# A retention layer followed by a bilinear feed-forward: how the first unit, w_out and the later loads are brought in

## The chip, the cores and the metric

The kernel runs on one core of a Trainium2 chip. The metric is the device time of one execution in microseconds (us); the median of 4 runs of the kernel before is 337.08 us (336.23 to 338.5). A core has five engines that run their own instruction lists and wait for each other by semaphores: PE (matrix products; its weight loads are shown as PEld), DVE and ACT (elementwise work), POOL (elementwise work, and here the issuer of nearly all loads) and SP (here the issuer of the stores and of transposes by DMA). PE's results stand in PSUM, which the program divides into eight banks, and other engines copy them out.

## The reference

For every batch b and head h, with q, k, v of 576 rows of 64 numbers (8 batches, 8 heads):

```python
scores = scale * np.matmul(q, k.transpose(0, 1, 3, 2))
Dmat = np.where(rel >= 0, gamma[:, None, None] ** rel[None, :, :], 0.0)
ret = scores * Dmat[None, :, :, :]
attn_out = np.matmul(ret, v)
x = attn_out.transpose(0, 2, 1, 3).reshape(4608, 512)
out = ((x @ w_a) * (x @ w_b)) @ w_out       # w_a, w_b: 512 x 1536, w_out: 1536 x 512
```

`rel` is the row minus the column, and gamma is 1 - 2^(-5-h). So each head is causal linear attention whose weight decays with distance, and its result goes through a feed-forward layer in which two products are multiplied with each other. Everything is float32 outside; the kernel computes in bfloat16 with float32 sums.

## The kernel before

The decay gamma^(row-column) is split into a factor for the row, put on q's side, and one for the column, put on v. A step of 64 rows then needs three things: its own masked scores times v, the state (the sum of k^T v over all earlier steps of the batch) times q, and the update of the state. Tokens are handled in chunks of 128 rows, in units of two chunks, and the feed-forward in blocks of 512 tokens: `ffn_ab` makes hT = (w_a x)(w_b x) by 12 slices F of d_ff (lines 414 and 422 are its products, 419 ACT's copy of the first, 427 DVE's multiplication), `ffn_out` multiplies hT with w_out (line 453) and stores the result.

The first 512 tokens, the "fresh" units 0 and 1 of 256 tokens each, have code of their own, for PE can do nothing before they are in. `load_fresh_qk` and `load_fresh_v` bring them in so that a partition holds two neighbouring tokens, called even and odd (`e`). For each unit PE transposes q and k (line 492), ACT and DVE copy them out of PSUM (614, 617, 618, 626, 630), PE makes the scores (549), DVE masks them with `keep2` (561), v is scaled with `vs_all` (`fresh_vscale`, line 479: for unit 0 on DVE in two halves of heads, for unit 1 on POOL), PE adds k^T v into `kv_sum` (`fresh_kv`, line 514), ACT copies that state (521), PE multiplies state with q (`fresh_from_state`, 527) and masked scores with v (`fresh_stage2`, 572), and xT is copied out (583, 586, 588). q's factor of unit 0 is `qs0`, four exponentials on ACT (206), multiplied in by DVE at line 614. `idle_products` are products of a tile of zeros that give PE something to do while it waits for loads, and `settled` is one such product that waits for a state.

The order on every engine is the order in which the program is written: nothing reorders it. POOL's list decides when loads start. It issues q, k and half of v of unit 0 (the other half is SP's), unit 1, w_a and w_b in slices of d_ff (`load_w`, 118), the whole of w_out (`load_wo`, 124) and then chunks 4 to 9 (`load_v` 110, `load_qk` 102). Loads to bfloat16 are converted on the way. A DMA issued by POOL waits for the landing of the eighth DMA that POOL issued before it.

Later units are woven into the feed-forward by a list `todo` of (cost, function, arguments). `run` adds up the cost of the feed-forward products (1.0 for a product 512 wide), and at each edge between groups calls what is due. `first` computes state times q and scores of a unit (`stage1`), `second` the rest (`stage2`), `kv` the state update (294), `transposes` the transposed q and k, on PE for chunks 4 to 7 (275, into a bank of the pool `ps_ffn`, which has 4 banks), by DMA from SP for the others. `ps_x` and `ps_o` have 2 banks each. `later` holds small steps that `pop` hands out one at a time.

## Time and profile before

| | |
|---|---|
| median of 4 runs | 337.08 us (336.23 to 338.5) |
| the profiled execution's own time | 335.46 us |
| its span, first to last instruction | 333.7 us |
| PE busy | 322.5 us, 97% of the span, 3746 products |
| DVE, POOL, ACT busy | 165.5, 143.6, 112.6 us |
| mean granted clock of PE | 0.993 |
| moved by DMA | 40.94 MB, mean 123 GB/s |
| product of 512 columns, start to start | 0.86 us for four |

The page of a profile cuts the span in 40 slices of 8.3 us and gives the busy share of each engine in tenths, and the clock that PE was granted. Its chain of waits is followed back from the last instruction. A line of the timeline is: start, duration of the merged run of instructions, engine, line of the kernel, operation, tile written and tiles read, shape, count, and in brackets how long the engine had been idle and what released it. A line of the waits is: who waited for whom, microseconds in total, times, and the longest.

### The profile page before, as it was taken

How to read it: one execution, taken by the hardware profiler on the slowest of the kernel's cores; microseconds unless marked ns; L12 is line 12 of the kernel's file. 1: busy time of each engine (PE TensorE's matmuls, PEld its weight loads, DVE VectorE, ACT ScalarE, POOL GpSimd, SP SyncE). 2: the span in 40 equal slices, each digit the busy share in tenths (PEclk: the TensorE clock that was granted, in tenths of full speed). 3: DMA queues.
4: the chain of work that ended last, by engine and by line, in shares of the span. 5: the costliest groups of instructions: out<-in, count | busy, mean ns of one | idle time of the engine just before them, and what ended most of it. 6: DMA issues, size and time to landing. Idle time of an engine off the chain costs nothing.

```text
span 333.7 us, 8838 instructions
## 1 busy us (share of the span) xinstructions
PE 322.5 (97%) x3746; PEld 166.9 (50%) x3746; DVE 165.5 (50%) x324; ACT 112.6 (34%) x233; POOL 143.6 (43%) x176
## 2 busy tenths in 40 slices
PE   6989989989999999999999999999999999999995
PEld 2664346877544454444444444454445444444443
DVE  6754345757643555446435644464455534444321
ACT  4737523545143214332333223322323133213321
POOL 8786298797666895308350855072000000000000
PEclk9799999999999999999999999999999999999999
DMA  9999999999999999907999599339801600020002
GB/s 140 206 154 194 217 190 242 175 127 173 187 230 165 125 133 214 173 5 101 109 200 102 87 148 251 24 65 137 181 0 33 128 34 1 17 81 31 2 31 94
DMA packets 116151, 40.94 MB, mean 123 GB/s; under 512 B 102992, under 2 KB 109392, under 8 KB 116112
## 3 DMA queue, kind: packets, MB, share of 16 engines
q0 software_dynamic: 80688, 23.34, 67.7%
q1 hardware_dynamic: 35280, 16.95, 26.6%
q8 instruction: 29, 0.48, 0.6%
q10 hardware_dynamic: 144, 0.10, 0.1%
q14 instruction: 10, 0.08, 0.1%
HBM read 37.75 MB, written 9.44 MB: 141 GB/s over the span
## 4 chain that ended last, share of the span: by engine, by line
PE 84%; DMA 10%; POOL 3%; issue 1%; DVE 0%; ACT 0%; POOLq 0%; ACTq 0%
PE po L453 26%; PE pa L414 25%; PE pb L422 25%; DMA wo_sb<-in_moe_w_out_dram 4%; DMA vf<-in_v_dram 2%; DMA wa_sb<-in_moe_w_a_dram 2%; PE o L339 2%; PE o L381 2%; PE kv L294 2%; DMA qk<-in_k_dram 1%; PE sc L359 1%; POOL fqk L141 1%; PE po L442 1%; POOL fvb L479 1%; POOL wb_sb L118 1%
## 5 line engine op out<-in xcount | busy, mean ns | idle before, releaser
L427 DVE TENSOR_TENSOR hT<-ha,pb 128x512 bf16<-128x512 bf16 (+1 forms) x123 | 76.5, 622 | 99.8 <-PE pb L422 84.6
L414 PE MATMUL pa<-xT,wa_sb 128*128 128x512 bf16 (+1 forms) x492 | 113.8, 353 | 1.6 <-issue 1.2
L422 PE MATMUL pb<-xT,wb_sb 128*128 128x512 bf16 (+1 forms) x492 | 113.5, 353 | 0.0
L419 ACT CAST ha<-pa 128x512 bf16<-128x512 f32 (+1 forms) x123 | 65.6, 533 | 123.9 <-PE pa L414 122.8
L453 PE MATMUL po<-wo_sb,hT 128*128 128x512 bf16 x420 | 95.5, 380 | 0.6 <-DMA wo_sb<-in_moe_w_out_dram 0.6
L422 PEld LDWEIGHTS <-wb_sb 128*128 128x128 bf16 x492 | 48.1, 98 | 45.3 <-issue 0.3
L414 PEld LDWEIGHTS <-wa_sb 128*128 128x128 bf16 x492 | 46.9, 98 | 46.1 <-issue 2.1
L256 POOL TENSOR_TENSOR vb<-vf,vs_all 128x512 bf16<-128x512 f32 x30 | 31.5, 1060 | 77.4 <-PE o L339 44.5
L453 PEld LDWEIGHTS <-hT 128*128 128x128 bf16 x420 | 39.1, 98 | 45.3 <-DMA wo_sb<-in_moe_w_out_dram 1.1
L462 ACT COPY osb<-po 128x512 f32<-128x512 f32 x18 | 10.5, 585 | 74.8 <-PE po L453 74.8
L102 POOL DMA_DIRECT2D qk<-in_q_dram x36 | 31.1, 868 | 6.7 <-DMA wo_sb<-in_moe_w_out_dram 6.2
L110 POOL DMA_DIRECT2D vf<-in_v_dram x36 | 31.9, 888 | 1.2 <-DMA wb_sb<-in_moe_w_b_dram 1.2
L102 POOL DMA_DIRECT2D qk<-in_k_dram x36 | 31.2, 874 | 0.6 <-DMA wa_sb<-in_moe_w_a_dram 0.4
L367 DVE TENSOR_TENSOR sT<-sc,keep 128x512 bf16<-128x512 f32 x32 | 20.6, 685 | 12.1 <-PE sc L359 12.1
L398 DVE TENSOR_TENSOR xT<-o,qs 128x512 bf16<-128x512 f32 x32 | 20.6, 685 | 11.9 <-PE o L339 11.8
L307 DVE TENSOR_TENSOR s<-kv,s 128x256 f32<-128x256 f32 x49 | 20.6, 420 | 5.9 <-ACT sbf L317 4.6
L317 ACT CAST sbf<-s 128x256 bf16<-128x256 f32 x56 | 21.1, 406 | 3.1 <-DVE s L305 2.7
L464 DVE COPY osb<-po 128x512 f32<-128x512 f32 x17 | 11.7, 687 | 19.3 <-PE po L453 19.3
L339 PE MATMUL o<-qkT,sbf 64*64 64x64 bf16 x456 | 12.1, 195 | 0.1
L339 PEld LDWEIGHTS <-sbf 64*64 64x64 bf16 x456 | 8.2, 107 | 5.7 <-issue 5.5
L381 PEld LDWEIGHTS <-vb 64*64 64x64 bf16 x512 | 6.4, 108 | 6.6 <-issue 6.6
L381 PE MATMUL o<-sT,vb 64*64 64x64 bf16 x512 | 8.2, 195 | 0.0
(75 smaller groups left out, 128.3 us busy)
## 6 DMA issues: line engine op xcount, KB each, us to landing
out_dram<-osb SPq DMA_DIRECT2D x35, 256.0 KB, 4.9
vf<-in_v_dram POOLq DMA_DIRECT2D x29, 256.0 KB, 6.2
qk<-in_q_dram POOLq DMA_DIRECT2D x28, 128.0 KB, 6.6
qk<-in_k_dram POOLq DMA_DIRECT2D x28, 128.0 KB, 6.9
wo_sb<-in_moe_w_out_dram POOLq DMA_DIRECT2D x1, 1536.0 KB, 14.3
wa_sb<-in_moe_w_a_dram POOLq DMA_DIRECT2D x6, 192.0 KB, 6.5
wb_sb<-in_moe_w_b_dram POOLq DMA_DIRECT2D x6, 192.0 KB, 7.3
vf<-in_v_dram POOLq DMA_DIRECT2D x8, 128.0 KB, 7.6
```

The costliest lines, as they stand in the source:

```text
L102: nc.gpsimd.dma_start(t[r0:r0 + n, w, :].rearrange("p (h d) -> p h d", h=H), src[b, :, s0:s0 + n, :].rearrange("h s d -> s h d"))
L110: nc.gpsimd.dma_start(t[r0:r0 + n, :].rearrange("p (h d) -> p h d", h=H), v[b, :, s0:s0 + n, :].rearrange("h s d -> s h d"))
L256: eng.tensor_tensor(vb.rearrange("p (h d) -> p h d", h=H), vf.rearrange("p (h d) -> p h d", h=H), vs[:, i % PER, :].unsqueeze(2).to_broadc ...
L307: nc.vector.tensor_tensor(new, ps[s][:, ci], last_sum[0], op=ALU.add)
L317: nc.scalar.copy(sb, new)
L339: nc.tensor.matmul(o[s][half(c), ci, j, :], st[half(r), p, :], qkt_of[i][half(r), 0, p, half(s)], start=start, stop=True, skip_group_check ...
L381: nc.tensor.matmul(o[s][half(c), ci, j, :], vb[half(s), 64 * h:64 * h + 64], sT[half(s), h % 2, ci, h // 2, :], start=False, stop=True, sk ...
L414: nc.tensor.matmul(pa[:, 0:n], wa_sb[:, c, fs], xT[:, c, tok0:tok0 + n], start=(c == 0), stop=(c == NC - 1))
L419: nc.scalar.copy(ha[:, 0:n], pa[:, 0:n])
L422: nc.tensor.matmul(pb[:, 0:n], wb_sb[:, c, fs], xT[:, c, tok0:tok0 + n], start=(c == 0), stop=(c == NC - 1))
L427: nc.vector.tensor_tensor(hT[:, F, off:off + n], ha[:, 0:n], pb[:, 0:n], op=ALU.mult)
L453: nc.tensor.matmul(po, hT[:, F, u * 128:(u + 1) * 128], wo_sb[:, F, :], start=(F == 0), stop=(F == NF - 1))
```

## The change

- q of unit 0 is loaded by SP as float32 into `fq32` and scaled to bfloat16 by DVE in two halves of heads, with row factors `qv` (16 numbers a partition, one exponential) in place of `qs0`. Its transposes are copied out in halves by ACT and DVE, without a factor.
- POOL's first DMA is k of unit 0, the second is all of v of unit 0. v's even part is scaled by POOL, its odd part by ACT in eight operations of one head each. For unit 1 the even part is DVE's and the odd part ACT's. On POOL's list the scaling stands between w_a and w_b of the first slice.
- `idle` is float32: 9 products of 512 columns become 2 of 512 and 1 of 128, and the later 1 and 2 become 1 of 128 and 1 of 256. `idle_beside` is new: two such products of 256 columns ahead of `fresh_kv(1, 0)`. Products with the zero state of unit 0 are left away.
- k of unit 1 is transposed after `fresh_kv(0, 1)` and copied in halves by ACT and DVE. The mask's row numbers come from POOL.
- w_out is loaded in three parts, with chunk 4 and chunk 5 between them; `ffn_out_parts` does block 0 in the same three parts and holds four banks of `ps_ffn`. Transposes of chunks 4 and 5 go to `ps_x`.
- The costs in `todo` change: chunk 4 is transposed earlier, `kv` of the third and fourth unit and the loads of chunks 10 to 13 come later.

```diff
+    fq32 = const.tile([128, 2 * DM], FP32)
...
+    def load_fresh_qk(u, w):
+        t = nat.tile([128, 2, DM], BF16, tag="qk", name="fqk")
+        flat = t.rearrange("p a b -> p (a b)")
+        if u == 0 and w == 0:
+            nc.sync.dma_start(fq32.rearrange("p (h x) -> p h x", h=H),
+                              fresh_src(w, u))
+        else:
+            nc.gpsimd.dma_start(flat.rearrange("p (h x) -> p h x", h=H),
+                                fresh_src(w, u))
+        fresh[u, w] = flat.rearrange("p (h e d) -> p h e d", h=H, e=2)
+        return flat
...
-    load_fresh_v(0, 0, 4, nc.sync)
-    load_fresh_qk(0)
+    load_fresh_qk(0, 0)
+    load_fresh_qk(0, 1)
     ramp(idx[:, 0:512], [[1, 512]], 0, 0)
     ramp(posf[:, 0:4], [[1, 2], [256, 2]], 0, 2)
     ramp(posf[:, 4:4 + MID + 1], [[128, MID + 1]], 0, 1)
-    load_fresh_v(0, 4, 8, nc.gpsimd)
+    for c in (0, 1):
+        ramp(rowf[64 * c:64 * c + 64, 0:2], [[1, 2]], 0, 2)
+    load_fresh_v(0, 0, 8, nc.gpsimd)
+    load_fresh_qk(1, 0)
     ramp(posf[:, 4 + MID + 1:NPOS], [[128, PER - MID - 1]], 64, 1)
-    load_fresh_qk(1)
+    load_fresh_qk(1, 1)
     load_fresh_v(1, 0, 8, nc.gpsimd)
-    load_w(0, 128)
-    load_w(128, 384)
-
-    idle = const.tile([128, 512], BF16)
+    load_w(0, 128, (0,))
+
+    idle = const.tile([128, 512], FP32)
...
-    qs0 = const.tile([128, HP, 256], FP32)
-    for p in range(HP):
-        nc.scalar.activation(qs0[:, p], idx[:, 0:256], AF.Exp,
-                             bias=biasq[:, 0:1], scale=lgq[:, p:p + 1])
+    qv = const.tile([128, 2, H], FP32)
+    nc.vector.tensor_tensor(
+        qv, posf[:, 0:4:2].unsqueeze(2).to_broadcast([128, 2, H]),
+        lgv.unsqueeze(1).to_broadcast([128, 2, H]), op=ALU.mult)
+    nc.scalar.activation(qv, qv, AF.Exp, bias=biasq[:, 0:1], scale=-1.0)
...
-    def transposes(i, by_dma):
+    def transposes(i, by_dma, place=ps_ffn, tag="ab"):
...
+    def ffn_out_parts(blk, parts):
+        hT = hT_of.pop(blk)
+        po = [ps_ffn.tile([128, 512], FP32, tag="ab", name="po")
+              for _ in range(4)]
+        for f0, f1 in parts:
+            for u in range(4):
+                for F in range(f0, f1):
+                    nc.tensor.matmul(po[u], hT[:, F, u * 128:(u + 1) * 128],
+                                     wo_sb[:, F, :],
+                                     start=(F == 0), stop=(F == NF - 1))
+                    if F < f1 - 1:
+                        yield 1.0, False
+                if f1 == NF:
+                    store(512 * blk + 128 * u, po[u], u)
+                pop()
+                yield 1.0, True
...
-        for e in (0, 1):
+        for e in es:
+            if eng is nc.scalar:
+                for h in range(h0, h1):
+                    nc.scalar.activation(
+                        fv[u][e][:, 64 * h:64 * h + 64],
+                        vf2[:, u, 128 * h + 64 * e:128 * h + 64 * e + 64],
+                        AF.Copy, bias=0.0,
+                        scale=vs_all[:, 2 * e + u, h:h + 1])
+                continue
...
-                fresh_from_state(u, h, s, j == 0)
+                if u or s:
+                    fresh_from_state(u, h, s, j == 0)
...
+    def idle_beside(n):
+        for _ in range(n):
+            nc.tensor.matmul(kv_sum[:, 256:512], idle[:, 0:128],
+                             idle[:, 0:256], start=False, stop=True,
+                             skip_group_check=True)
...
-    idle_products(9)
-    fresh_vscale(0, 0, 4, nc.vector)
+    idle_products(2)
+    idle_products(1, 128)
+    make_qs(256, 512)
+    make_keep2()
+    for h0 in (0, 4):
+        nc.vector.tensor_tensor(
+            fresh[0, 0][:, h0:h0 + 4],
+            fq32.rearrange("p (h e d) -> p h e d", h=H, e=2)[:, h0:h0 + 4],
+            qv.rearrange("p e h -> p h e")[:, h0:h0 + 4].unsqueeze(3)
+            .to_broadcast([128, 4, 2, D]), op=ALU.mult)
     q_out, k_out = fresh_tiles(0)
-    tq = fresh_transposed(0, 0, 0, HP, AB)
-    idle_products(1)
+    tq = [fresh_transposed(0, 0, 0, 2, AB), fresh_transposed(0, 0, 2, 4, X)]
+    idle_products(1, 128)
+    nc.scalar.copy(q_out[:, 0:2], tq[0].rearrange("p c e t -> p c t e"))
+    nc.vector.tensor_copy(q_out[:, 2:4], tq[1].rearrange("p c e t -> p c t e"))
     tk = [fresh_transposed(0, 1, 0, 2, AB), fresh_transposed(0, 1, 2, 4, X)]
-    make_keep2()
-    nc.vector.tensor_tensor(q_out, tq.rearrange("p c e t -> p c t e"),
-                            qs0.rearrange("p c (t e) -> p c t e", e=2),
-                            op=ALU.mult)
     nc.scalar.copy(k_out[:, 0:2], tk[0])
     nc.vector.tensor_copy(k_out[:, 2:4], tk[1])
-    make_qs(256, 512)
-    idle_products(2)
-    fresh_vscale(0, 4, 8, nc.vector)
+    fresh_vscale(0, 0, 8, nc.gpsimd, (0,))
+    fresh_vscale(0, 0, 8, nc.scalar, (1,))
+    load_w(0, 128, (1,))
+    load_w(128, 384)
+    idle_products(1, 256)
     fresh_scores(0, (X, AB))
     fresh_kv(0, 0)
     q_out, k_out = fresh_tiles(1)
     tq = fresh_transposed(1, 0, 0, HP, AB)
     nc.scalar.copy(q_out, tq.rearrange("p c e t -> p c t e"))
-    tk = fresh_transposed(1, 1, 0, HP, AB)
     fresh_state1(0)
     fresh_kv(0, 1)
-    nc.scalar.copy(k_out, tk)
-    fresh_vscale(1, 0, 8, nc.gpsimd)
+    tk = [fresh_transposed(1, 1, 0, 2, AB), fresh_transposed(1, 1, 2, 4, X)]
+    nc.scalar.copy(k_out[:, 0:2], tk[0])
+    nc.vector.tensor_copy(k_out[:, 2:4], tk[1])
...
     fresh_stage2(0)
+    fresh_vscale(1, 0, 8, nc.vector, (0,))
+    fresh_vscale(1, 0, 8, nc.scalar, (1,))
     fresh_scores(1, (X, O))
     run_all(ffn_ab(0, 0, 256, 0, 1))
+    idle_beside(2)
     fresh_kv(1, 0)
...
-    load_wo(0, NF)
...
-    load(*range(4, 10))
-    todo = [(110, vscale, (4, nc.vector)), (110, vscale, (5, nc.vector)),
-            (110, transposes, (4, False)), (112, transposes, (5, False)),
+    PARTS = ((0, 4), (4, 8), (8, NF))
+    load_wo(*PARTS[0])
+    load(4)
+    load_wo(*PARTS[1])
+    load(5)
+    load_wo(*PARTS[2])
+    load(*range(6, 10))
+    todo = [(90, vscale, (4, nc.vector)),
+            (90, transposes, (4, False, ps_x, "x")),
+            (108, vscale, (5, nc.vector)),
+            (112, transposes, (5, False, ps_x, "x")),
             (116, kv, (units[0], nc.scalar)),
             (128, first, (0,)), (136, second, (0,)),
-            (136, vscale, (6, nc.gpsimd)), (136, vscale, (7, nc.gpsimd)),
-            (142, transposes, (6, False)), (148, transposes, (7, False)),
-            (152, kv, (units[1], nc.scalar)),
+            (136, vscale, (6, nc.gpsimd)), (142, vscale, (7, nc.gpsimd)),
+            (144, transposes, (6, False)), (150, transposes, (7, False)),
+            (154, kv, (units[1], nc.scalar)),
             (174, first, (1,)), (184, second, (1,)),
-            (150, transposed, (2,)), (151, scale_v, (2,)),
-            (152, load, (10, 11)),
-            (184, kv, (units[2], nc.scalar)),
-            (191, transposed, (3,)), (192, scale_v, (3,)),
-            (193, load, (12, 13)),
-            (207, kv, (units[3], nc.scalar)),
-            (232, first, (2,)), (244, second, (2,))]
+            (146, transposed, (2,)), (165, scale_v, (2,)),
+            (178, load, (10, 11)),
+            (194, kv, (units[2], nc.scalar)),
+            (206, transposed, (3,)), (214, scale_v, (3,)),
+            (216, load, (12, 13)),
+            (218, kv, (units[3], nc.scalar)),
+            (236, first, (2,)), (246, second, (2,))]
...
-    run(ffn_out(0))
+    run(ffn_out_parts(0, PARTS))
```

## The prediction

> **What bounds the kernel now.** First the page, for where PE is not busy. PE is at nine tenths or more from the fifth slice of 8.3 us on, bar two; the chain that ended last is PE for 84%, DMA for 10%. So the time is PE's work plus PE's waits, and only two stretches have waits: the first 24 us, and 38 to 68 us.
>
> ```profile
> PE   6989989989999999999999999999999999999995
> PEclk9799999999999999999999999999999999999999
> ...
> PE 84%; DMA 10%; POOL 3%; issue 1%; DVE 0%; ACT 0%; POOLq 0%; ACTq 0%
> ```
>
> Second PE's waits, then PE's timeline around the three that stand after 24 us.
>
> ```profile
> PE pa L414 <- issue: 1.2, 1, 1.2
> ...
> PE tp L275 <- DMA qk<-in_k_dram: 1.1, 1, 1.1
> PE po L453 <- DMA wo_sb<-in_moe_w_out_dram: 0.6, 1, 0.6
> ...
> 38.36 1.03 PE L422 MATMUL pb<-xT,wb_sb 128*128 128x512 bf16 x4
> 40.03 3.63 PE L453 MATMUL po<-wo_sb,hT 128*128 128x512 bf16 x16 [0.65 <-DMA wo_sb<-in_moe_w_out_dram]
> 43.49 1.12 PE L275 MATMUL tp<-identity,qk 128*128 128x128 bf16 x12
> 45.70 0.40 PE L275 MATMUL tp<-identity,qk 128*128 128x128 bf16 x4 [1.09 <-DMA qk<-in_k_dram]
> ...
> 66.46 0.50 PE L414 MATMUL pa<-xT,wa_sb 128*128 128x256 bf16 x3
> 68.18 0.28 PE L414 MATMUL pa<-xT,wa_sb 128*128 128x256 bf16 x1 [1.21 <-issue]
> ```
>
> Idle time is counted from a modelled end; the loss is read from start to start. Four 512-wide matmuls start every 0.86 us, so the first po was due at 39.22 and came at 40.03: 0.8 lost. Four transposes take 0.22, so the last four were due at about 44.4 and came at 45.70: 1.3. At 66.46 three of four matmuls run and the fourth, due at 66.8, comes at 68.18: 1.4, with no releaser. Sum 3.5 us.
>
> Why were the loads late? POOL's timeline: the q load of chunk 5 is issued only when w_out, one DMA of 1536 KB, has landed. The queue holds eight DMAs, and the whole of w_out sat in one place.
>
> ```profile
> 33.22 0.91 POOL L110 DMA_DIRECT2D vf<-in_v_dram  x1 [1.02 <-DMA wb_sb<-in_moe_w_b_dram]
> 40.28 0.88 POOL L102 DMA_DIRECT2D qk<-in_q_dram  x1 [6.16 <-DMA wo_sb<-in_moe_w_out_dram]
> ```
>
> The 1.4 us: the page lists 29 packets, 0.48 MB, on queue q8 "instruction", 16 KB each, against 7,492 rows of PE and PEld: one packet for some 258 rows. In the packet list one starts at 65.6 and takes 1.25, just ahead of the hole. PE had gone through the 256 rows before it in 3.3 us (a state product and two groups of 64x64 products stand close together there), the shortest such stretch of the trace.
>
> Last the prologue, by windows of the clock's own steps (columns: stretch, length, busy us of PE, PEld, DVE, ACT and POOL, granted clock, DMA share, GB/s).
>
> ```profile
> 5.00:8.42 3.42, 1.58 (x34) 1.02 (x33) 2.83 (x8) 1.44 (x3) 3.42 (x5) 1.00 1.63 216
> 8.42:11.83 3.41, 3.41 (x74) 2.36 (x70) 2.68 (x6) 2.93 (x6) 2.90 (x6) 0.50 1.55 247
> 11.83:15.24 3.41, 2.69 (x113) 2.11 (x112) 1.76 (x4) 2.81 (x4) 1.98 (x3) 1.00 1.53 188
> ```
>
> A stretch with PE 46% busy is followed by one at half clock. The profiled execution took 335.46 us: span 333.7 and 1.8 around it. The median of the runs is 337.08, 1.6 more; I carry differences over to the median unchanged.
>
> **The change part by part.** All times are us from the span's start.
>
> *q, and scores of unit 0.* Before, SP's 256 KB of v landed 2.9 after an issue at 0.74; its packets ran 1.3 of that. Twice the bytes: 4.9, and 0.3 for sharing with k from 3.5 on: 5.2. DVE then scales q in two operations of 0.69 (row L256, same shape): halves at 5.9 and 6.5. k, now POOL's first DMA (row L141: 5.1 from an issue at 1.26, so 6.4), pays 0.5 for q's share: 6.9. Transposes of k 0.70, a copy 0.59: scores at about 8.4 instead of 9.57. This gain of 1.2 is worth nothing by itself: v is late next. Gone from ACT's way are four qs0 exponentials (0.49 each) and from DVE's the 1.23 of L614; they hid behind DMAs.
>
> *v of unit 0.* It is second on POOL. Its 512 KB follow k by 1.3 (twice the 0.6 by which 256 KB of v trailed k, 8.0 to 8.6) to 2.0 (unit 1: k 11.5, v 13.5): 8.2 to 8.9; I take 8.6. Even parts go to POOL: one L479 operation, 1.05, begun 0.3 after landing (L118 at 13.81 after 13.53): done at 9.95. Behind this wait on POOL's queue stand the issues of wb(0:128), wa and wb(128:384), and all weights after them; they have cover, since POOL's two operations on unit 1's v (14.44 to 16.49) go, and the load of wa(384:768) starts near 14.5, not 16.43. Odd parts go to ACT: eight activations 128x64. Nearest row: L235 128x64, two in 0.77, start to start 0.34, with two pointer operands; L200 128x32 with none takes 0.23 against 0.43. The new ones have one, so halfway, 0.26 each, 2.1 in all (bounds 0.16 and 0.34: 1.3 and 2.8): done at 10.75. The last product of kv(0,0) ends at 10.85, before it was 11.05: **-0.2**. From there to the first pa the steps keep their rows; eight zero-state products of 0.02 go.
>
> *v of unit 1.* pa and pb of F=0 end 5.3 after kv(0,0) (16.37-11.05), at 16.15. Before, kv(1,0) began at 16.45. Now DVE scales the even part (0.69, hidden), ACT the odd part in 2.1 after its copy of xT (14.93 before, 14.7 now): 16.8. PE itself first runs two idle_beside products. No fp32 product is in the trace: from one bf16 product of that width (0.11) to, by the column counts that the diff trades (512 bf16 columns for 128 fp32), four (0.43). I take four, the dearer end for this sum: 0.86, PE there at 17.0. **+0.5** for kv(1,0) and all behind it. Prologue's bounds: -0.15 (v at 8.2, activations at 0.16) to +1.65 (v at 8.9, activations at 0.34 in both units).
>
> *The other idle products.* 9x512 become 2x512 and 128 in fp32, and the later 1x512 and 2x512 become 128 and 256: at four each the same fill. They end near 5.3, before q's first half: 0. If dearer, 0.6 is covered.
>
> *w_out in thirds, chunks 4 and 5 between.* Weights end near 30.2 (32.2 before, minus 2.0). A third is 2.5 (512 KB at the 207 GB/s of 34 to 38 us), a chunk's loads 2.7 (39.98 to 42.73). So third 1 lands at 32.7, chunk 4 at 35.4, third 2 at 37.9, chunk 5 at 40.6, third 3 at 43.1. PE asks at about 39.7 for the first two, 43.7 for chunk 5, 44.3 for third 2, 48.4 for third 3: 2.8 or more to spare. **-0.8 and -1.3.** The three extra issues are 1.0 each of POOL, hidden under DMA time. The four po banks are held until the last third; their copies (0.59, 0.69) end 0.9 after it, and the fourth bank is needed 1.3 after.
>
> *Transposes of 4 and 5 in ps_x.* kv of unit 4,5 now needs that bank. In before the copies ended 1.47 after the transposes began (45.70 to 47.17); kv comes 1.3 after: **+0.3** (0 to 0.6).
>
> *Rows of PE.* kv of units[2] goes from 184 to 194, out of second(1)'s edge, and some 35 rows fewer precede it. The 256 rows at the old hole then take about 5.6 by the rows' durations, the shortest elsewhere 4.3: **-1.4** (0 if the hole only moves).
>
> *Loads held back.* POOL's order of instructions there is unchanged, so 0 (plus or minus 0.3).
>
> Sum: -0.2-0.8-1.3+0.3-1.4 with the +0.5 in place of the -0.2: 0.5-0.8-1.3+0.3-1.4 = **-2.7**; 335.46 becomes 332.8, the median 337.08 becomes **334.4**.
>
> **Two rules weighed.** The Trainium skill, "TensorE: Matmul & The Clock Gate", Part 1, has the clock fall after one idle window of about 3.4 us. Here it fell after a window 46% busy, so the row decides. By the rule neither kernel loses anything after 5 us; by the row a thin window costs, which is the second rival.
> "Runtime: NRT & Kernel Launch", Instruction fetch mechanics, has blocks of 256 instructions, their cost mostly hidden. By the rule the hole at 66.8 is no fetch and stays, and the sum would be -1.3.
>
> **The rivals.**
> 1. *v late.* v at 8.9 and activations at 0.34: the prologue is +1.65, total -1.55: 335.5. For it: v now queues behind k. Against: half the pointers. 0.09.
> 2. *The clock, the slower end.* Between scores and kv(0,0) PE now waits for v; 8.42 to 11.83 holds only about 1.7 of work, as thin as the window that cost before. Half clock in 11.83 to 15.24 costs 2x2.69-3.41 = 2.0, in the next (2.95 busy) 2.5. One window: 336.4, 0.05. Two: 338.9, 0.18. It decides from two windows on, and comes sooner if an fp32 product fills less than four bf16 ones. Against: the middle of the prologue is dense.
> 3. *The hole only moves.* Sum -1.3: 335.8. 0.07.
> 4. *More.* The runs' 1.6 above the profile may be half-clock time that the added fill spares: 332.8. 0.10.
>
> **How the numbers follow.** Forecast 0.51, own range 333.0 to 335.8. About 0.5% (1.7 us: below 335.4, above 338.8) is what a measurement of this kernel can tell from no change. Faster: 0.44 of the forecast, 0.10 of more, 0.02 of the moved hole, 0.03 of v late: 0.59. Slower: 0.17 of two windows. Same: the rest, 0.24. The range holds the forecast, late v, the moved hole and one window, and reaches to two windows: 332.5 to 339.0.
>
> **What would show it.** Right: po's first wait and tp's wait on k gone from PE's waits; no 1.2 "issue" at pa; scores near 8.4; kv(0,0) waiting on ACT and ending near 10.9; kv(1,0) near 17.0. Wrong: granted 0.50 in windows after 11.8; activations of 0.34; v landing past 9; po waiting for a third of w_out; a new "issue" hole of over 1 us.

## The result: no difference, and the profile after

The changed kernel takes 337.9 us (median of 54 runs, 334.07 to 345.52), the kernel before 336.52 (78 runs, 334.69 to 342.67). The ratio is 1.0005, with an interval of 0.9989 to 1.0022: no difference is shown. The ratios, and the table below, leave out executions more than 1.5% above the fastest of the same kernel (16 of these 54; of the runs below, from none of p's twelve to five of e's and m's), so 1.0005 is not the ratio of the two medians, which is 1.004. 334.4 was forecast, 2.7 less than before. The profiled execution of the changed kernel is one of its long ones (343.71 us, span 341.9), so its waits are also read in a second profile of the same kernel, run a below (339.83 us, span 338.1).

From the page after: PE's slices, its granted clock and the chain that ended last.

```profile
PE   7689999989879999999999999999999999999996
PEclk9899999999969999999999999999999999999999
...
PE 80%; DMA 12%; POOL 4%; issue 2%; ACT 1%; DVE 0%; POOLq 0%; ACTq 0%
```

Of the dents of before, the one in the slice at 42 to 50 us is gone; the one at 67 to 75 us is still there (now 68 to 77). A new one stands at 85 to 103 us, and the chain has more DMA (12% instead of 10%) and POOL (4% instead of 3%). Next PE's waits (who waited for whom, us in total, times, the longest).

```profile
PE kv L297 <- DMA qk<-in_k_dram: 3.3, 2, 2.2
PE kv_sum L546 <- POOL fvb L511: 2.6, 1, 2.6
PE kv L297 <- issue: 1.6, 1, 1.6
...
PE sc L362 <- DVE s L310: 0.6, 1, 0.6
```

`po` no longer waits for w_out and `tp` no longer for k; in their place `kv` waits for a k, `sc` for DVE, unit 0's state update for POOL's scaling, and the wait without a releaser has a new instruction. PE's timeline shows where.

```profile
42.42 0.61 PE L278 MATMUL tp<-identity,qk 128*128 128x128 bf16 x8
42.87 3.62 PE L451 MATMUL po<-wo_sb,hT 128*128 128x512 bf16 x16
46.33 0.61 PE L278 MATMUL tp<-identity,qk 128*128 128x128 bf16 x8
...
69.64 0.34 PE L297 MATMUL kv<-vb,qk 64*64 64x64 bf16 x9
71.57 0.32 PE L297 MATMUL kv<-vb,qk 64*64 64x64 bf16 x15 [1.58 <-issue]
...
82.12 0.44 PE L362 MATMUL sc<-qkT 64*64 64x64 bf16 x30 [0.64 <-DVE s L310]
...
93.60 0.32 PE L297 MATMUL kv<-vb,qk 64*64 64x64 bf16 x16 [1.10 <-DMA qk<-in_k_dram]
96.08 0.42 PE L297 MATMUL kv<-vb,qk 64*64 64x64 bf16 x16 [2.17 <-DMA qk<-in_k_dram]
96.44 1.89 PE L482 MATMUL po<-wo_sb,hT 128*128 128x512 bf16 x4
```

Eight transposes, sixteen products, eight transposes follow each other without a gap: the 2.1 us of before are gained. Then the hole (1.78 from start to start), now inside `kv` of the third unit, 0.84 at the scores, and 3.3 of waiting at `kv` of chunks 14 and 15. The last line is a second loss: four products take 1.89 and not 1.03, since the clock was granted at half from 94.83 to 101.66.

**Where the executions differ.** Each run lists the granted clock of the execution. A window of 3.41 us at half clock takes 0.005 off the mean, so the windows that an execution lost can be counted. Not counted is the half clock at the start (in r nine products of 512 columns take 4.02), which ended between 4.4 and 10.0 us in the profiles. Of the executions that the ratios rest on (the changed kernel with run a; the kernel before beside all runs), medians in us:

| windows at half clock | before | changed |
|---|---|---|
| none | 336.1 (74 of 150) | 335.5 (9 of 46) |
| one | 336.5 (46) | 336.9 (19) |
| two | 336.8 (9) | 337.6 (17) |
| more | 336.8 to 339.4 (21) | 339.0 (1) |

At full clock the changed kernel's median is 0.6 lower, but its nine executions range from 334.07 to 338.15, so this 0.6 is not clear of their scatter. It runs at full clock in 20% of these executions and the kernel before in 49%, and its medians rise by 1.4 and 0.7 with the first and second window. So there are two questions: why not 2.7 at full clock, and why the clock falls more often.

### The profile page after: what moved, and what is told of

The parts are those of the page before. It is cut to its first block, busy times and chain, and to the rows that moved or that the text cites. A ratio compares the mean times of both kernels' runs of the same rounds, so it can differ in the third digit from the quotient of the medians.

```text
span 341.9 us, 8833 instructions
## 1 busy us (share of the span) xinstructions
PE 327.1 (96%) x3740; PEld 170.0 (50%) x3740; DVE 164.8 (48%) x313; ACT 114.8 (34%) x247; POOL 143.3 (42%) x178
## 4 chain that ended last, share of the span: by engine, by line
PE 80%; DMA 12%; POOL 4%; issue 2%; ACT 1%; DVE 0%; POOLq 0%; ACTq 0%
PE pa L417 24%; PE pb L425 24%; PE po L482 23%; DMA vf<-in_v_dram 9%; DMA qk<-in_k_dram 3%; POOL qk L102 2%; PE o L342 1%; PE o L384 1%; PE kv L297 1%; PE po L451 1%; POOL vf L110 1%; PE sc L362 1%; PE po L471 1%; POOL vb L259 1%; ACT fvb L505 1%
## 5 line engine op out<-in xcount | busy, mean ns | idle before, releaser
L430 DVE TENSOR_TENSOR hT<-ha,pb 128x512 bf16<-128x512 bf16 (+1 forms) x123 | 76.5, 622 | 100.8 <-PE pb L425 88.3
L482 PE MATMUL po<-wo_sb,hT 128*128 128x512 bf16 x372 | 86.8, 388 | 0.0
L482 PEld LDWEIGHTS <-hT 128*128 128x128 bf16 x372 | 35.3, 100 | 41.5 <-issue 3.3
L440 DVE COPY osb<-po 128x512 f32<-128x512 f32 x17 | 11.7, 687 | 22.1 <-PE po L482 21.1
L297 PE MATMUL kv<-vb,qk 64*64 64x64 bf16 x448 | 8.0, 197 | 4.9 <-DMA qk<-in_k_dram 3.3
L451 PE MATMUL po<-wo_sb,hT 128*128 128x512 bf16 x48 | 11.2, 380 | 0.0
```

The source lines that it names most:

```text
L430: nc.vector.tensor_tensor(hT[:, F, off:off + n], ha[:, 0:n], pb[:, 0:n], op=ALU.mult)
L482: nc.tensor.matmul(po, hT[:, F, u * 128:(u + 1) * 128], wo_sb[:, F, :], start=(F == 0), stop=(F == NF - 1))
```

## The experiments

All ratios are to the kernel before, run on the same chip in the same session, with a 95% interval.

| run | edit | median | ratio |
|---|---|---|---|
| a | the changed kernel again | 338.15 | 1.0043 (1.0008 to 1.0078) |
| b | before, w_out in thirds alone | 337.6 | 0.9971 (0.9926 to 1.0015) |
| c | the new prologue alone | 337.39 | 1.0017 (0.9984 to 1.0050) |
| d | changed, later list as before | 338.27 | 1.0028 (0.9996 to 1.0060) |
| e | b, loads of chunks 14, 15 early | 338.5 | 0.9973 (0.9932 to 1.0015) |
| f | changed, loads of chunks 14, 15 early | 335.89 | 0.9992 (0.9951 to 1.0033) |
| g | changed, more fill before the first state update | 336.34 | 0.9971 (0.9937 to 1.0005) |
| h | changed, without `idle_beside` | 335.7 | 0.9940 (0.9908 to 0.9972) |
| i | h, w_b before POOL's scaling | 337.72 | 0.9969 (0.9921 to 1.0017) |
| j | i, loads of chunks 14, 15 early | 336.97 | 0.9981 (0.9936 to 1.0026) |
| k | h, PE's list shifted | 340.76 | 1.0072 (1.0029 to 1.0116) |
| l | i, later list as before | 336.51 | 0.9968 (0.9925 to 1.0011) |
| m | k, loads of chunks 14, 15 early | 339.18 | 1.0024 (0.9979 to 1.0070) |
| n | m, with `idle_beside` | 338.84 | 1.0041 (1.0003 to 1.0079) |
| o | h again, another chip | 336.44 | 0.9977 (0.9936 to 1.0017) |
| p | changed, two state updates later | 338.13 | 1.0060 (1.0023 to 1.0097) |
| q | k, two state updates later | 337.35 | 1.0028 (0.9991 to 1.0065) |
| r | b, two state updates later | 335.98 | 0.9956 (0.9917 to 0.9994) |

### First four: the parts by themselves

**a**, the changed kernel unaltered.

> The changed kernel once more, for a profile and for its time beside the three others. The theory 'v late in the prologue' expects 0 to +1 us against the kernel before, with the first 512-wide pa 1.5 to 3 us later than the 23.7 of before, and the waits on w_out and on chunk 5's k gone. The rival 'later loads held back' expects a wait of kv on a load of k of 1 to 3 us between 85 and 100 us; if that wait is missing here, it is not what sets the median.

**b**, the kernel before with `ffn_out_parts`, w_out's three loads and the first five entries of the new list.

```diff
-    run(ffn_out(0))
+    run(ffn_out_parts(0, PARTS))
```

> The kernel before with only w_out in thirds, chunks 4 and 5 between them, ffn_out_parts and the transposes in ps_x. Both theories expect the 0.8 and 1.3 us of waits at 39 to 46 us to go and 0 to 0.3 to come: 1.8 to 2.1 us faster than before, unless the four stores that now leave together delay later loads, which a third theory says; that one expects a gain under 0.7 us and landings of chunks 10 and 11 some 4 us later.

**c**, the changed kernel with w_out in one load, `ffn_out(0)` and the list of before.

```diff
-    run(ffn_out_parts(0, PARTS))
+    run(ffn_out(0))
```

> The changed kernel's prologue with the rest of before (w_out in one load, ffn_out, the list of before). 'v late' expects 1.5 to 3 us slower than before. 'Held back' expects no difference, within 0.7 us. The hole without a releaser at 66.8 us should move or close, since some 35 rows of PE fewer stand ahead of it.

**d**, the changed kernel with the list's later entries at the costs of before.

```diff
-            (146, transposed, (2,)), (165, scale_v, (2,)),
-            (178, load, (10, 11)),
-            (194, kv, (units[2], nc.scalar)),
...
+            (150, transposed, (2,)), (151, scale_v, (2,)),
+            (152, load, (10, 11)),
+            (184, kv, (units[2], nc.scalar)),
```

> The changed kernel with the later entries of the list (units 2 and 3, chunks 10 to 13) at the costs that they had before. 'v late' expects the time of the changed kernel within 0.7 us. 'Held back' expects it 1.5 to 3 us faster than the changed kernel, with chunks 12 and 13 issued 4 us or more earlier and no wait of kv on k.

PE's timeline in b: the gain stands, and a wait for chunk 15's k undoes it in the profiled execution.

```profile
39.82 3.62 PE L448 MATMUL po<-wo_sb,hT 128*128 128x512 bf16 x16
43.27 0.61 PE L275 MATMUL tp<-identity,qk 128*128 128x128 bf16 x8
...
92.99 0.32 PE L294 MATMUL kv<-vb,qk 64*64 64x64 bf16 x16 [4.05 <-DMA qk<-in_k_dram]
```

A second wait in b, 1.58 at 69.9 us, stands where a hole had been expected; its releaser is the k of chunk 11. In c the same `kv` waits 2.4 though w_out is as before, after a first state update that comes late:

```profile
PE kv_sum L546 <- POOL fvb L511: 2.5, 1, 2.5
PE kv L297 <- DMA qk<-in_k_dram: 2.4, 1, 2.4
```

In d no `kv` waits for k and `sc` does not wait, but the hole, at `pa` now, is the longest of all:

```profile
66.12 0.27 PE L417 MATMUL pa<-xT,wa_sb 128*128 128x256 bf16 x1
69.58 0.73 PE L417 MATMUL pa<-xT,wa_sb 128*128 128x256 bf16 x3 [3.18 <-issue]
```

What follows: no part alone is shown to be faster or slower; a, the whole, is 0.4% slower in its session. The prologue is later in all four profiles of it (the first 512-wide `pa` at 24.9 to 26.9; 23.7 before, 23.8 in b), and later waits come and go.

### Why the prologue is later

**g**, two more products of zeros where PE waits for v.

```diff
     fresh_scores(0, (X, AB))
+    idle_products(2, 256)
     fresh_kv(0, 0)
```

> The changed kernel with two more products of zeros, float32 and 256 columns, between the scores of unit 0 and its first state update. Theory (PE waits there for v, and the thin window is paid with half clock afterwards): no granted 0.50 in 11.7 to 18.8, where three profiles of this prologue had one window and one had two; the first state update starts at 10.4 to 10.9 where v is in time (10.05 before this edit), and the first 512-wide pa at 23.5 to 24.5 in place of 24.9 to 26.9; ratio to the changed kernel 0.994 to 0.997. Rival (64x64 products count as thin whatever stands before them): half clock in 11.7 to 15.1 stays and the first 512-wide pa is at 25.5 or later.

**h**, the two products ahead of the second unit's state update taken away; **o**, the same kernel again.

```diff
     run_all(ffn_ab(0, 0, 256, 0, 1))
-    idle_beside(2)
     fresh_kv(1, 0)
```

> The changed kernel without the two products of zeros ahead of the second unit's first state update. Theory (they cost 0.9 to 1.5 by the profiles, and nothing else is late there, for ACT has scaled the odd part by then): the first 512-wide pa 0.6 to 1.0 earlier at the same clock. Rival 1 (ACT's eight scalings end later than pb): the state update waits for ACT and the gain is under 0.3. Rival 2 (they hold the clock): a granted 0.50 between 15 and 22 us that the changed kernel did not have there, and the first pa later by 1 or more.

> The changed kernel without the two products of zeros, a second time on another chip. Theory (0.9 of PE's time and no more, the rest of the first result was an execution at full clock): ratio 0.995 to 0.999, with an interval that reaches 0.994; in the profile no half clock or one window, and where there is one the first 512-wide pa at 24 to 25. Rival (the products cost 2 us, for they bring a second window at half clock): 0.992 to 0.995 again.

**i**, also w_b's first slice ahead of POOL's scaling.

```diff
+    load_w(0, 128, (1,))
     fresh_vscale(0, 0, 8, nc.gpsimd, (0,))
     fresh_vscale(0, 0, 8, nc.scalar, (1,))
-    load_w(0, 128, (1,))
     load_w(128, 384)
```

> The changed kernel without the two products of zeros ahead of the second unit's first state update, and with the two loads of w_b's first slice put on POOL's list ahead of its scaling of v, not behind it. Theory (both things that the first pa and pb of the prologue paid are gone): no wait of pb on w_b (0.7 in one profile of the changed prologue), the first 512-wide pa at 23.2 to 23.6 wherever the clock stays at 1.00, ratio to before 0.992 to 0.995, as without the products alone or 0.1 better. Rival (the gain of taking the products away was a lucky clock): half clock in 11 to 19 us, the first 512-wide pa at 24.5 or later, ratio 0.998 to 1.002.

**l**, i with the later list of before, as in d.

> The changed kernel without the two products of zeros, with w_b's first slice ahead of POOL's scaling, and with the list's later entries (units 2 and 3, chunks 10 to 13) at the costs of the kernel before. Theory (holding them back costs 0.8 at the scores of the third unit, which wait for DVE, and now and then a wait of kv on k of chunks 14 and 15): no wait of sc on DVE's sums, no wait of kv on a DMA between 85 and 97, and 0.5 to 1.5 less time than with the costs of the changed kernel. Rival (those costs only trade one wait for another): a hole without a releaser of 1.4 to 3.5 at 64 to 67 us, and no less time.

Run f (its edit stands below, and is at 64 us and later) has the changed prologue at full clock throughout. PE's timeline in f: `pb` waits for w_b, the load whose issue had been put behind POOL's scaling, then the two products run, then the state update.

```profile
14.92 0.61 PE L417 MATMUL pa<-xT,wa_sb 128*128 128x256 bf16 x4
16.25 0.61 PE L425 MATMUL pb<-xT,wb_sb 128*128 128x256 bf16 x4 [0.72 <-DMA wb_sb<-in_moe_w_b_dram]
16.70 1.03 PE L639 MATMUL kv_sum<-idle 128*128 128x256 f32 x4
17.66 0.44 PE L546 MATMUL kv_sum<-fvb,fqk 64*64 64x64 bf16 x16
```

In h the same place has neither, and no wait for ACT's scaling took their place:

```profile
15.60 0.60 PE L425 MATMUL pb<-xT,wb_sb 128*128 128x256 bf16 x4
16.13 0.55 PE L546 MATMUL kv_sum<-fvb,fqk 64*64 64x64 bf16 x16
```

From `pb` to the state update: 1.41 in f, 0.53 in h, so the two products cost 0.88. The first 512-wide `pa` is at 24.87 in f and 23.42 in h; the other 0.57 is w_b. That part is luck between executions: in h the issue of w_b stands at the same place, but it landed at 15.20, just ahead of `pb`, and in f at 16.21. In i that wait is gone, but POOL's scaling then stands behind two issues, and the first state update starts at 10.7 and not at 10.1: `pa` at 23.9. Moving w_b only trades one lateness for another.

Then the clock. The windows of the clock's own steps (columns: stretch, length, busy us of PE, PEld, DVE, ACT and POOL, granted clock, DMA share, GB/s), first of a, then of f, then of g:

```profile
8.61:12.02 3.41, 2.35 (x84) 1.75 (x78) 2.48 (x4) 2.64 (x10) 3.06 (x5) 1.00 1.47 235
12.02:15.43 3.41, 3.23 (x77) 2.52 (x72) 1.06 (x3) 2.38 (x6) 1.37 (x3) 0.50 1.46 180
15.43:18.85 3.42, 3.40 (x27) 2.52 (x25) 3.38 (x7) 2.02 (x8) 3.42 (x7) 0.50 1.02 131
```

```profile
8.13:11.55 3.42, 2.48 (x76) 1.65 (x76) 2.65 (x5) 2.49 (x10) 3.05 (x5) 1.00 1.52 182
11.55:14.96 3.41, 2.71 (x106) 2.01 (x105) 1.55 (x3) 3.00 (x7) 1.69 (x4) 1.00 1.43 222
14.96:18.37 3.41, 2.42 (x29) 1.59 (x28) 2.88 (x6) 1.82 (x8) 3.41 (x8) 1.00 1.27 170
```

```profile
6.87:10.29 3.42, 3.33 (x58) 2.33 (x57) 2.45 (x5) 1.24 (x5) 1.99 (x4) 1.00 1.32 152
10.29:13.70 3.41, 2.50 (x68) 1.93 (x68) 1.28 (x3) 2.94 (x10) 3.41 (x6) 1.00 1.44 251
13.70:17.11 3.41, 3.11 (x71) 2.25 (x71) 1.93 (x4) 2.55 (x9) 2.06 (x4) 0.50 1.34 154
```

a and f run the same program up to 64 us. PE is busy for 2.35 of a window in a and two at half clock follow (`pa` at 26.49); for 2.48 in f and none follows. The windows start anew in each execution (at 8.61 and at 8.13 here), so the same work is cut in other places. In g the window that the fill makes dense is followed by one with 2.50 busy, and that one by half clock, so its expectation failed in the profile (`pa` at 27.60). Over executions g does better than the changed kernel: 6 of the 10 that its ratio rests on were at full clock, against 9 of 46. Ten are few, and it is not taken as shown.

PE's busy share does not sort these windows, but a count that the traces allow does. Give each product the time of its columns at full clock (0.86 us for four of 512, twice that for each product recorded as float32), times the part of the 128 by 128 array that its line names (`64*64` a quarter, `128*64` half), and divide the sum by the window. Over all 20 profiles, the last 5 us left out, 1846 windows ran at full clock. 18 of them come to less than 0.33, and each is followed by half clock (before at 5.00: 0.31; a at 8.61: 0.30; g at 10.29: 0.328; k at 89.97: 0). 1822 come to more than 0.37, and none is. Of the six between, at 0.34 to 0.35, two are (n, o) and four are not (a, b, f, q). Products of zeros are counted in. The new prologue comes nearer to the fall: its thinnest stretch of 3.41 us between 6.5 and 20 us, the small products around the wait for v, holds 0.03 to 0.32 in eleven profiles of it (0.25 in f and h; seven traces lack some 40 of PE's products and are left out here), and that of the old one 0.31 in e and 0.39 in before. No edit was made to test this count, so it is a reading of the traces and not a shown cause.

What follows: `idle_beside` costs its 0.88 and h is the better kernel. The interval of the first run lies below 1, o's reaches from 0.9936 to 1.0017. Of both runs together, h at full clock has a median of 334.0 (7 executions, 333.17 to 336.36), the changed kernel 335.5, before 336.1. In l, as in d, `sc` does not wait, and the hole is long (2.44).

### The hole

**k**, one float32 product of the start replaced by 64 small ones that take about its time.

```diff
-    idle_products(2)
+    idle_products(1)
     idle_products(1, 128)
+    for _ in range(64):
+        nc.tensor.matmul(kv_sum[:, 0:64], idle_bf[:, 0:128],
+                         idle_bf[:, 0:64], start=True, stop=True,
+                         skip_group_check=True)
```

> The changed kernel without the two products of zeros ahead of the second unit's first state update, with one float32 product of 512 columns at the start (recorded as two weight loads and two products) replaced by 64 bfloat16 products of 64 columns, so that all later work stands 62 recorded weight loads further down PE's list. Theory (the hole without a releaser is PE waiting for the next part of its instruction list, at a fixed place of the list: after 857 recorded weight loads in seven profiles, 61 later in one): the kv of the third unit, at 66 to 70 us, runs without the hole of 0.9 to 1.8, and if a hole stays it begins after 857 weight loads, which is now in the second stage of the second unit or ahead of it, 3 us earlier; the time between 0.0 and 1.4 below the same kernel without the shift. Rival 1 (something that this kv needs is late): the hole stays at the 25th product of the kv. Rival 2 (a fixed moment, where the transfers are densest): a hole at the same 66 us whatever runs there.

Counted in the trace, the hole begins after the 857th recorded weight load of PE in before, a, c, d, f, g, h, i, j, l, o, p, r and the changed kernel, whatever stands there: `pa` in before, c, d and r, `pb` in l, and in the others a product of `kv`: after the ninth with the changed prologue, after the fifth in g, whose fill records four weight loads more, and after the thirteenth where the four of `idle_beside` are gone, as in h:

```profile
66.18 0.37 PE L297 MATMUL kv<-vb,qk 64*64 64x64 bf16 x13
67.25 0.28 PE L297 MATMUL kv<-vb,qk 64*64 64x64 bf16 x11 [0.70 <-issue]
```

Its length goes with the instruction packet that moves at that time:

| | packet runs | hole, start to start | from packet's end |
|---|---|---|---|
| before | 65.60 to 66.85 | 66.69 to 68.18 | 1.3 |
| changed | 68.86 to 70.04 | 69.79 to 71.57 | 1.5 |
| d | 66.92 to 68.22 | 66.12 to 69.58 | 1.4 |
| h | 65.00 to 66.00 | 66.36 to 67.25 | 1.2 |
| r | 63.38 to 64.46 | 65.29 to 65.83 | 1.4 |

PE goes on 1.2 to 1.5 after the packet's end; a packet that starts late makes a long hole (3.45 in d), an early one a short one (0.54 in r). The two kernels with no hole there and no shift fit as well: in b the packet had ended at 62.86 and PE came at 64.34, in e it ended at 63.41 and PE went on at 64.75 after 0.33. With 62 weight loads more in front (k, m, n, q) there is no hole: in k a packet ended at 60.86 and PE came to the place, now in the second stage of the second unit, at 64.37. All of `kv` runs through at 67.44:

```profile
67.44 0.44 PE L297 MATMUL kv<-vb,qk 64*64 64x64 bf16 x24
...
89.52 0.32 PE L297 MATMUL kv<-vb,qk 64*64 64x64 bf16 x16 [1.02 <-DMA qk<-in_k_dram]
93.77 0.43 PE L297 MATMUL kv<-vb,qk 64*64 64x64 bf16 x16 [3.94 <-DMA qk<-in_k_dram]
```

Other holes without a releaser keep the same distance from a packet: one in e and one in r after 223 weight loads (1.4 after the packet's end), one in m and one in o after 1240 and 1239 (1.5 and 1.2). In o a packet ran from 87.84 to 89.28:

```profile
90.50 0.42 PE L297 MATMUL kv<-vb,qk 64*64 64x64 bf16 x29 [1.06 <-issue]
```

From 223 to 857 and on to 1239 there are 1268 and 764 rows of PE and PEld, near five and three of the packets of some 258 rows. The hole is PE waiting for its own instructions. (b, said to have it 61 loads later, has a wait for k there, as shown above.) But k is slower, by 0.7%: the same fence shows `kv` of chunks 14 and 15 waiting 5.0, and none of the 11 executions that its ratio rests on was at full clock. That taking the hole away saves time is not shown: q, with neither hole nor wait for a load, took 333.9 and 334.6 in its two executions at full clock, and h, with a hole, 334.0.

### Where PE waits for late loads

**e** (to b) and **f** (to the changed kernel) issue the loads of chunks 14 and 15 earlier, at cost 216 and 220; **j** and **m** do it to i and k, **n** is m with `idle_beside`.

```diff
             (218, kv, (units[3], nc.scalar)),
+            (220, load, (14, 15)),
...
-            if g + 3 < len(units):
+            if 2 < g < len(units) - 3:
                 load(*units[g + 3])
```

> w_out in thirds alone (the kernel before, with block 0's last product and chunks 4 and 5 as in the changed kernel), and the loads of chunks 14 and 15 put on POOL's list at cost 216, ahead of the scaling of chunks 12 and 13, instead of behind it at 232. Theory (the gain at 39 to 46 us is given back by a wait of the state update on k of chunks 14 and 15, whose loads POOL issues only after it has waited for an earlier v): no wait of kv on a DMA between 85 and 97 us where w_out in thirds alone had 5.6; the hole without a releaser stays, 1.3 to 1.8, near 69.7. With 2.1 gained and nothing given back 334.5 against 336.5, ratio 0.994. Rival (the DMA rings are full there whatever the order of issue): the wait moves to another load, at least 2 us, ratio 0.998 to 1.001.

> The changed kernel with the loads of chunks 14 and 15 put on POOL's list at cost 220, right behind kv of the fourth unit, instead of in the first stage of the third unit at 236. Theory (that wait and a later prologue eat the gain): the waits on k near 92 us, 2.4 and 3.3 in two profiles, go; the first 512-wide pa stays at 24.9 to 26.9; ratio to before 0.999 (gain 2.1, prologue 1.2 to 3.2 and about 0.8 of a wait at sc given back), and 2.4 below the changed kernel. Rival (the prologue alone is the reason): no change against the changed kernel, 1.003.

> The kernel before this one in the list, and the loads of chunks 14 and 15 on POOL's list at cost 220 instead of behind the scaling of chunks 12 and 13 at 236. Theory (the wait of the state update on k of chunks 14 and 15 stands in some executions of the changed kernel and is gone with the loads earlier): no wait of kv on a DMA between 85 and 97, the ratio to before equal to the one without the early load or up to 0.5% lower. Rival (the scaling of v, now behind six more issues on POOL, comes late): kv waits for POOL's vb by 1 or more near 74 to 80, and the ratio is higher by 0.2% or more.

> The kernel with the shifted list and without the two products of zeros, and the loads of chunks 14 and 15 at cost 220 in place of 236 as in the run that had the early load alone. Theory (the shift takes the hole away, but PE then comes to the state update of chunks 14 and 15 before their k, which landed 1.4 ahead of PE in the kernel before; with both the gain is kept): no hole at 64 to 70, kv of chunks 14 and 15 waits under 1 (5.4 with the shift alone), ratio to before 0.988 to 0.993, and 1.0 to 1.7% under the shift alone. Rival 1 (the transfers are the limit up to 134 us whatever the order): the wait moves to a later state update or to POOL's scaling, 2 or more between 80 and 125, ratio 0.998 or more. Rival 2 (the shift itself costs, by what stands at the start): the first 512-wide pa later than 24.5 at full clock.

> The changed kernel with its two products of zeros kept, the list shifted and the loads of chunks 14 and 15 at cost 220. Theory (of the 2.7 that the change was to bring, the hole gave 1.4 less, and the wait for k took 2.4 to 3.3): hole and wait gone, what is left is the later prologue, 1.2 at full clock and 3 with two windows at half clock, so ratio 0.993 to 0.998 against before. Rival (the prologue alone decides): ratio 1.000 to 1.004, as for the changed kernel.

**p**, **q** and **r** leave the loads and let PE come later.

```diff
-        if 4 <= g + 2 < len(units):
+        if 6 <= g + 2 < len(units):
             kv(units[g + 2], nc.scalar)
...
+    todo += [(290, kv, (units[4], nc.scalar)),
+             (330, kv, (units[5], nc.scalar))]
```

> The changed kernel with the state updates of chunks 12, 13 and of 14, 15 taken out of the second stages of the third and fourth unit and put at costs 290 and 330, so that PE comes to them 9 and 12 us later; their sums are first needed at costs 368 and 402. Nothing is loaded earlier. Theory (the gain is eaten where PE, now earlier, meets loads that are not earlier): no wait of kv on a DMA or on POOL between 80 and 100, and ratio 0.994 to 0.999 against before, since 2.1 is gained at 39 to 46 and the prologue gives 1.2 to 3.2 back. Rival (the transfers bound all of the first 134 us): the wait moves to transposes or scores of the next units, 2 or more between 90 and 134, and the ratio stays at 1.000 to 1.004.

> The kernel with the shifted list and without the two products of zeros, and the same two state updates at costs 290 and 330. Theory: neither hole (0.9 to 1.8) nor a wait of kv on a load (5.0 with the shift alone), so 331.5 to 333.5 in an execution, ratio 0.986 to 0.992, against 1.007 with the shift alone. Rival: a wait of 2 or more elsewhere before 134 us, ratio 0.998 or more.

> The kernel before with w_out in thirds alone, and the same two state updates at costs 290 and 330. Theory: the 5.6 that kv waited for k in the profile with w_out in thirds alone is gone, and the gain of 2.1 stays whole, ratio 0.991 to 0.995. Rival (that wait was no part of the time, since the executions without it are no faster): ratio 0.996 to 0.999 as before.

PE's timeline of before, a line that the prediction did not use:

```profile
90.18 0.50 PE L294 MATMUL kv<-vb,qk 64*64 64x64 bf16 x32
```

Chunk 15's k had landed at 88.8, so the slack was 1.4. In the profiles with a wait (changed, a, b, c, k) PE was there between 88.3 and 92.4, and k landed at 96.0, 94.9, 92.9, 93.7 and 93.7. So k came 4 to 7 us later than before. PE came earlier than before only in b and k (88.6 and 88.3); in the changed kernel, a and c it came later (91.0 to 92.4) and waited all the same. POOL's timeline after tells why the load was late: POOL scales v of chunk 10 and then of chunk 11, whose load it issued at 60.23, waits for each, and only then issues the loads behind them.

```profile
60.23 0.91 POOL L110 DMA_DIRECT2D vf<-in_v_dram  x1
...
66.29 1.04 POOL L259 TENSOR_TENSOR vb<-vf,vs_all 128x512 bf16<-128x512 f32 x1 [3.40 <-DMA vf<-in_v_dram]
72.03 1.04 POOL L259 TENSOR_TENSOR vb<-vf,vs_all 128x512 bf16<-128x512 f32 x1 [4.71 <-PE kv L297]
```

That v of chunk 11 landed at 71.9, 11.7 after its issue (the line's releaser, `kv`, ended at the same time). Before it took 6.0, and in the other runs 5.5 to 12.4. The issue at 60.23 was as early as before (60.33). In f no `kv` waits for k; but neither does one in d, g, h, i, l and o, whose loads are not early, so f does not show that the early load is why, and j's ratio does not differ from i's. In n a wait stands at POOL's scaling of chunks 12 and 13 instead, now behind six more issues (1.3 in m, 4.3 in e):

```profile
87.21 0.43 PE L297 MATMUL kv<-vb,qk 64*64 64x64 bf16 x16 [4.85 <-POOL vb L259]
```

In p, q and r no `kv` waits for a load or for POOL. Instead `sc` of a later unit waits 0.9 for DVE at 109 to 112 us, for the sums now come just ahead of it. All three profiles pay it: p is 0.6% slower than before (2 of its 12 executions were at full clock), and q, without the hole, forecast at 0.986 to 0.992, is at 1.0028 with an interval that takes in 1. r is 0.4% faster, with an interval that ends at 0.9994; at full clock it stands at 334.4 (3 executions).

What follows: w_out in thirds takes its two waits away in every profile. In time that shows only in r, where `kv` meets no late load, and there by little; b and e, with intervals that take in 1, do not show it. That this wait alone eats the gain in the changed kernel is not borne out: p takes it away, at a price of 0.9, and is no faster. The first rival of m, a wait that only moves, held in n and e (5.4 and 4.3); in m what it moved was 1.3, less than the rival's 2.

## Why the prediction was wrong, step by step

Three terms of the sum failed: the hole, taken to close (-1.4), stayed; the loads held back, taken at 0, brought a wait at the scores and, in some executions, one for k; and the second unit (+0.5) was too small. Beside the sum, half clock was given 0.23 and came in 37 of 46 executions.

*The scaling of unit 0, -0.2.* Right where v is in time: it landed at 8.6 to 8.8 in a, d, f and h (8.6 taken), ACT's eight scalings took 2.02 (2.1 taken), and the first state update started at 9.84 to 10.07. In two of the first five profiles with this prologue (changed, c) one of sixteen parts of v landed 2 us after the others (10.6, 10.4), and the update came at 11.6 to 11.8. v after 9, named as a sign that would make it wrong, did come.

*The second unit, +0.5: mis-sized where w_b is late.* It was +1.2 in f and d, and +2.7 to +3.2 in a, c and the changed kernel. The working had `idle_beside` at 0.86 (measured 0.88) and ACT's scaling hidden. What failed is the sentence that the issues behind POOL's wait "have cover": w_b's first slice stands there, and in f `pb` waited 0.72 for it. Without that wait the term is near: h plus the 0.88 of the products makes 24.3, +0.6. The rest in a, c and the changed kernel is half clock and the late v. (The upper bound of the prologue, +1.65, is too low by the prediction's own steps: with v at 8.9 and activations at 0.34 ACT would end unit 1's odd part near 18.3, +1.9.)

*w_out in thirds, -0.8 and -1.3.* Right: both waits are gone in every profile with it. The second was a little larger than read: chunk 5's q held the transposes up by 0.3 ahead of its k, so 1.5 were lost there and not 1.3. *ps_x, +0.3.* About 0.1: `kv` starts 1.4 after the last transposes.

*The hole, -1.4: failed.* The prediction took it for an instruction fetch, which k bears out, but argued from the durations of 256 rows that it would close. It stayed, 0.9 to 2.4 from start to start in the kernels with the changed list against 1.48 before: the place in the list is fixed, and the change put `kv` on it. The third rival, "the hole only moves", was the right one for this step.

*Loads held back, 0 plus or minus 0.3: failed.* POOL's order is unchanged, as the step says, but the step took from this that nothing else moves. `sc` waits for DVE's sums in each profile with the changed list (0.84 from start to start; none in d and l, with the costs of before). And the order does not fix the landings: chunk 11's v took 11.7 and not 6.0, POOL waited for it before it issued chunks 14 and 15, and their k came past a slack of 1.4, a number that was in the trace of before. Why the same load takes so much longer in some executions stays open.

The sum at full clock, from the profile of f: prologue +1.2, thirds -2.1, `ps_x` +0.1, hole -0.2, scores +0.8, in all -0.2; f's span is 333.4 against 333.7. The wait for k, which f does not have, comes on top where it stands: 3.3 in the changed kernel, 2.4 in a.

*The clock.* The second rival priced one window at 336.4 in all and two at 338.9, and gave them chances of 0.05 and 0.18. The mechanism was right, the chance was not: 37 of 46 executions lost a window. That the medians (336.9 and 337.6) lie near these prices is partly luck: a window cost 1.4 and 0.7, not 2.0 and 2.5, on a base that was 1.1 higher than forecast. The prediction's rule, that a window PE leaves thin is followed by half clock, fails when thin means little busy time: windows with 55 to 64% busy were followed by full clock in b, e and i, and windows with 69 to 83% by half clock in a, d, g, n and o. It holds with the count above, by the part of the array that the products use. "TensorE: Matmul & The Clock Gate" of the Trainium skill, Part 1, has the clock fall after a whole idle window of about 3.4 us. One such window is in these traces (k, 89.97 to 93.38), and half clock followed it; but it followed those 69 to 83% as well, so the rule does not cover them. Why the changed kernel falls more often is made likely by the count and not shown.

"Runtime: NRT & Kernel Launch" of the skill, Instruction fetch mechanics, has fetches mostly hidden. Here that fits most of the page's 29 packets; the one at the 857th weight load costs up to 3.3, and e, m, o and r show another that costs 0.3 to 1.3.

## What to carry to other kernels

Where transfers are dense, look up in the trace of before how much slack the next waits have, and set it against how much the landing of one and the same load varies between executions: here 1.4 us of slack met a load that took 5.5 to 12.4. A wait there can bring the clock down on top (changed: half clock from 94.83). Fill that hides a wait costs its whole length wherever the wait is not there, so it is tried without (0.88 here). Compare executions by their granted clock before a sum of steps is called wrong or right.

## What had not been expected of the hardware

- A gap of PE that no semaphore explains stood at the same place of the instruction list, after 857 weight loads, in fourteen of twenty profiles, of kernels with different work there, and ended 1.2 to 1.5 us after an instruction packet had moved. 62 more weight loads in front left no gap.
- A float32 product of 256 columns costs 0.44 us, as four of bfloat16, and is recorded as two products and two weight loads.
- One of a load's sixteen parts can land 2 us after the rest, and the time from issue to landing of chunk 11's v went from 5.5 to 12.4 us between runs.
- Half clock followed every full-clock window of 3.41 us in which the products, weighted by the part of the array that they use, filled less than 0.33 of it, and none in which they filled more than 0.37; PE's busy share told the two apart only below 0.42 (always half clock) and above 0.83 (never).
- The windows of the clock start at another moment in each execution, so that the same program lost none, one or two of them in its first 20 us.
